# Turning q and k of seven head pairs on VectorE instead of TensorE, with a new order of short steps, in a block-sparse attention and Fourier-mixing kernel

## The chip, the cores and the metric

One Trainium2 chip, one NeuronCore. The time is the device time of one execution in microseconds (us). Most executions of one kernel lie within half a per cent of each other here: 42 of 44 runs of the kernel before in the four later jobs took 1108.34 to 1114.02 us at a granted TensorE clock of 0.991 to 0.995 of full speed; the two others took 1117.04 and 1117.07 us at 0.986. The kernel before had medians from 1109.45 to 1111.34 us on the chips of different jobs. So the clock differs a little from run to run, and kernels are compared by ratio: the mean time of one kernel's fast runs over that of the other's of the same rounds, which is not quite the ratio of the medians quoted beside it. A trace is of one execution, not always a typical one.

## The reference, cut to what matters

Four batches, eight heads, 768 positions, 64 features a head. Attention with a block mask (blocks of 32), then over the joined heads a two-dimensional Fourier transform of which the real part is added, a normalisation, and two dense layers with a relu.

```python
scores = scale * np.matmul(q, k.transpose(0, 1, 3, 2))   # q, k: (4, 8, 768, 64)
scores = np.where(mask, scores, -1e9)
attn = softmax(scores)                                   # rows; cut
x = np.matmul(attn, v)                                   # heads joined: (4, 768, 512)
u = x + np.real(np.fft.fft(np.fft.fft(x, axis=1), axis=2))
un = (u - mu) / np.sqrt(var + 1e-06)
out = u + np.maximum(un @ w_ch1, 0.0) @ w_ch2
```

## The kernel before: the parts that matter here

Two heads make a pair; there are 16 pairs, four a batch. A pair takes six steps (slots) of two score tiles each. While pair n is weighed, q and k of pair n + 1 are turned so that the features lie on partitions: twelve TensorE transposes into one shared PSUM bank ("t"), then copies. From the second batch on, the dense layers of the batch before fill the gaps of TensorE.

```python
def turn(n, a, half):                    # a: 0 for q, 1 for k
    ...
    for c, part in enumerate(parts):
        nc.tensor.transpose(tp[:, c * P:(c + 1) * P], part, ident)
    done = busy("PE", 0.15 * len(parts)) + HOP
    if a == 1:
        nc.scalar.copy(out=dst[:, half * HS:(half + 1) * HS], in_=tp[:, 0:HS])
        ...
    else:                                # q is put in the order even/odd, forward/backward
        for i, (to, to_jump, frm, jump, cnt, step) in enumerate(_TURNED[half]):
            on, copy = (("DVE", nc.vector.tensor_copy) if n == 0 and (half == 1 or i % 2 == 0)
                        else ("ACT", nc.scalar.copy))
            copy(out=_grid(dst, to, 2, to_jump, cnt, 1), in_=_grid(tp, frm, 2, jump, cnt, step))
```

The program is written out in advance against a small model of each engine's time (`when`, `free`, `busy`). Short steps (turns, copies of results, sums) wait in a list. `gap` takes those which the model holds ready; what is left is forced at the end of a slot.

```python
def slot(sl):
    ...                                  # scores, exponentials, values, products with gap()
    while short and (s in (2, 5) or len(short) > 1 or phase == 0 or sl == B * SB):
        short.popleft()[2]()             # first come, first served, ready or not
    ...                                  # loads of q and k
    w_steps(sl)                          # weight rounds of ACT and VectorE
```

## Time and profile before

| | value |
|---|---|
| time | 1109.45 us (1108.4 to 1109.46, 3 runs) |
| TensorE busy | 96% of the span; 99% from 300 to 1100 us |
| VectorE, ScalarE, GpSimd busy | 60%, 36%, 25% |
| TensorE at half clock in the trace | 16.2 us in four stretches, the last at the end |

A group's line gives source line, engine, operation, output and input with their shapes, count, then busy us and mean ns of one. PE is TensorE, PEld its weight loads, DVE is VectorE, ACT ScalarE, POOL GpSimd. In a timeline a line gives start, length, engine and group, and in brackets how long the engine stood idle before it and what ended that.

This is how the second half of pair 0's q (18.09) and of pair 1's q (22.90) is turned in the kernel before.

```profile
18.09 0.44 PE L447 MATMUL tp<-ident,qr 128*128 128x128 f32 x2 [1.12 <-ACT qT L456]
...
18.56 0.56 DVE L456 COPY qT<-tp 128x128 f32<-128x128 f32 x3 [7.51 <-PE tp L447]
...
20.63 0.43 DVE L414 TENSOR_SCALAR wraw<-wraw 128x512 uint32<-128x512 uint32 x1 [1.51 <-ACT wraw L413]
...
22.90 0.44 PE L447 MATMUL tp<-ident,qk 128*128 128x128 f32 x2
...
23.27 0.92 PE L478 MATMUL s<-qT,kT 64*128 64x384 f32 x4
```

VectorE copies q out of the bank at once (18.56) and starts on the weight round only after that (20.63); when TensorE comes to its next transposes the bank has long been free, and the line at 22.90 has no idle time before it.

### The profile page before, as it was taken

Reading aid. Unit: us, or ns where it says so; the run is one execution under the profiler, and the core shown is the slowest. Engines: PE = TensorE matmul, PEld = TensorE weight load, DVE = VectorE, ACT = ScalarE, POOL = GpSimd, SP = SyncE. Lnnn points to the kernel's source line nnn. Section 1 sums busy time; section 2 is a strip of 40 time slices with the busy share of each in tenths; the row PEclk is TensorE's granted clock in tenths of the full one; section 3 lists DMA queues with packets and bytes.
Section 4 is the critical chain, followed back from the end, with each engine's and each line's share of the span. In section 5 each row is a group of like instructions: output and inputs, shape, how many; then the busy total and the mean of one; then the engine's idle time right before and its main releaser. Section 6 shows DMA issues by size and latency. Waiting matters only on the chain.

```text
span 1109.3 us, 12468 instructions
## 1 busy us (share of the span) xinstructions
PE 1067.7 (96%) x4446; PEld 544.5 (49%) x4446; DVE 664.8 (60%) x1216; ACT 394.1 (36%) x818; POOL 274.2 (25%) x302
## 2 busy tenths in 40 slices
PE   8999988998899999999999999999999999999996
PEld 3333333544455545444444555454444555568675
DVE  5888878497754525653459355544356446575563
ACT  6788755555212102353443212244330202120210
POOL 1000088688100001245537000344540000000000
PEclk9999999999999999999999999999999999999999
DMA  7756311011000000211110000111000000100001
GB/s 219 208 176 215 93 51 43 15 45 42 1 1 1 0 1 19 66 33 27 43 29 15 1 0 1 51 50 29 1 1 0 1 1 19 39 1 1 1 16 45
DMA packets 65187, 44.30 MB, mean 40 GB/s; under 512 B 52814, under 2 KB 57948, under 8 KB 65116
## 3 DMA queue, kind: packets, MB, share of 16 engines
q1 hardware_dynamic: 63228, 42.62, 13.7%
q10 hardware_dynamic: 1856, 0.79, 0.3%
q8 instruction: 37, 0.61, 0.2%
q14 instruction: 34, 0.28, 0.1%
q0 software_dynamic: 32, 0.01, 0.0%
HBM read 37.11 MB, written 6.29 MB: 39 GB/s over the span
## 4 chain that ended last, share of the span: by engine, by line
PE 85%; DVE 9%; ACT 2%; issue 2%; DMA 0%; POOL 0%; SPq 0%; ACTq 0%; DVEq 0%; POOLq 0%
PE y L954 23%; PE z L898 15%; PE s L478 10%; PE o L522 9%; PE yp L898 7%; PE yy L1017 6%; PE xp L898 4%; DVE e L499 2%; PE tp L447 2%; PE zp L711 1%; PE sp L569 1%; PE zp L682 1%; PE xt L540 1%; PE s L483 1%; PE utp L823 1%
## 5 line engine op out<-in xcount | busy, mean ns | idle before, releaser
L509 POOL TENSOR_TENSOR acc<-acc,e 128x384 f32<-128x384 f32 x192 | 198.3, 1066 | 90.6 <-DVE e L499 90.1
L499 DVE TENSOR_TENSOR e<-s,mask 128x768 f32<-128x768 f32 x144 | 131.2, 951 | 78.4 <-ACT s L497 78.0
L478 PE MATMUL s<-qT,kT 64*128 64x384 f32 x768 | 161.7, 526 | 8.5 <-DVE e L499 7.4
L522 PE MATMUL o<-e,vr 128*64 128x384 f32 x768 | 145.1, 499 | 0.0
L497 ACT ACTIVATE s<-s 128x768 f32<-128x768 f32 x144 | 109.3, 795 | 65.5 <-PE s L478 64.9
L957 DVE TENSOR_TENSOR x<-y,x 128x512 f32<-128x512 f32 x72 | 49.8, 691 | 133.9 <-PE y L954 133.8
L954 PE MATMUL y<-w_sb,hB 128*128 128x512 f32 x288 | 128.4, 595 | 1.1 <-DVE x L957 1.0
L954 PE MATMUL y<-w_sb,hA 128*128 128x512 f32 x288 | 128.8, 594 | 0.6 <-ACT zs L713 0.6
L509 POOL TENSOR_TENSOR acc<-e 128x384 f32<-128x384 f32 x48 | 51.8, 1100 | 231.3 <-DVE e L499 173.2
L903 DVE TENSOR_TENSOR hA<-z,hA 128x384 f32<-128x384 f32 x64 | 35.7, 558 | 111.4 <-PE z L898 111.4
L478 PEld LDWEIGHTS s<-qT,kT 64*128 64x128 f32 x768 | 63.1, 187 | 68.1 <-DVE e L499 25.3
L898 PE MATMUL z<-unT,t 128*128 128x384 f32 x256 | 93.0, 486 | 0.0
L774 POOL TENSOR_SCALAR st<-st 128x1 f32<-128x1 f32 x24 | 6.6, 276 | 344.5 <-DVE st L773 344.1
L954 PEld LDWEIGHTS y<-w_sb,hB 128*128 128x128 f32 x288 | 53.3, 190 | 64.7 <-issue 62.1
L522 PEld LDWEIGHTS o<-e,vr 128*64 128x64 f32 x768 | 46.6, 136 | 73.9 <-issue 71.4
L954 PEld LDWEIGHTS y<-w_sb,hA 128*128 128x128 f32 x288 | 52.9, 190 | 59.6 <-issue 56.6
L907 ACT ACTIVATE hA<-hA 128x384 f32<-128x384 f32 x64 | 33.5, 524 | 123.6 <-DVE hA L903 123.1
L898 PEld LDWEIGHTS z<-unT,t 128*128 128x128 f32 x256 | 48.6, 190 | 33.9
L907 ACT ACTIVATE hB<-hB 128x384 f32<-128x384 f32 x64 | 33.6, 525 | 85.6 <-DVE hB L903 85.6
L898 PE MATMUL z<-t,w_sb 128*128 128x384 f32 x128 | 48.0, 499 | 3.1 <-DVE t L860 3.1
L898 PE MATMUL xp<-unT,w_sb 128*128 128x384 f32 x128 | 47.1, 491 | 1.5 <-ACT zs L713 1.1
L898 PE MATMUL yp<-unT,w_sb 128*128 128x384 f32 x128 | 46.7, 488 | 0.2 <-DVE un L747 0.2
(190 smaller groups left out, 1395.1 us busy)
## 6 DMA issues: line engine op xcount, KB each, us to landing
wraw<-in_moe_w_ch_dram SPq DMA_DIRECT2D x32, 512.0 KB
qr<-in_q_dram SPq DMA_DIRECT2D x90, 64.0 KB
vr<-in_v_dram SPq DMA_DIRECT2D x30, 192.0 KB
kr<-in_k_dram SPq DMA_DIRECT2D x28, 192.0 KB
out_dram<-x SPq DMA_DIRECT2D x16, 128.0 KB
out_dram<-x SPq DMA_DIRECT2D x8, 256.0 KB
out_dram<-x SPq DMA_DIRECT2D x8, 126.0 KB
out_dram<-x SPq DMA_DIRECT2D x4, 252.0 KB
```

The lines of the kernel that those rows point to most:

```text
L447: nc.tensor.transpose(tp[:, c * P:(c + 1) * P], part, ident)
L478: nc.tensor.matmul(s[:, i, 0:HS], kT[D * i:D * i + D, c * P:(c + 1) * P], qT[D * i:D * i + D, half * HS:(half + 1) * HS], start=True, stop ...
L497: nc.scalar.activation(out=s[:, :, 0:HS], in_=s[:, :, 0:HS], func=ACT.Exp, scale=scale)
L499: nc.vector.tensor_tensor(out=e, in0=s[:, :, 0:HS], in1=m.broadcast_to([P, 2, HS]), op=ALU.mult)
L509: nc.gpsimd.tensor_add(out=acc, in0=e_of[u - 1][:, i, :] if c == 1 else acc, in1=e[:, i, :])
L522: nc.tensor.matmul(o[D * i:D * i + D, :], vt[:, i, c, :], e[:, i, :], start=(c == 0), stop=(c == C - 1))
L898: nc.tensor.matmul(to, a[:, k, :], c[:, k, :], start=(k == 0), stop=(k == ND // 2 - 1))
L903: tt(out=to, in0=ps, in1=a, op=ALU.add)
L907: nc.scalar.activation(out=h, in_=h, func=ACT.Relu)
L954: nc.tensor.matmul(y, hs[0, half][:, l, m * P:(m + 1) * P], w2_sb[:, 4 * r + l, :], start=(l == 0), stop=(l == 3))
L957: nc.vector.tensor_tensor(out=x[:, m, :], in0=y, in1=x[:, m, :], op=ALU.add)
L1017: nc.tensor.matmul(ps, a[:, k, :], c[k // 2][:, k % 2, :] if isinstance(c, list) else c[:, k, :], start=(k == 0), stop=(k == 3))
```

## The change

Intent: take 84 transposes and their PSUM copies off TensorE and ScalarE. For pairs 9 to 15, q and k are loaded in blocks of 32 features by 32 positions (runs of 128 bytes), VectorE transposes the blocks in place, ScalarE puts q in order, and the scores read k with a stride of six columns. Beside that the first scores' copies all go to ScalarE, four warm-up matmuls are added, and short steps are taken in the order in which the model holds them ready. A limit with which the program compares the largest sum of squares also goes from 400 to 200. The core of the diff, with cuts marked:

```diff
+    BY_VECTOR = 2 * NP + 1
+    def load_blocks(n, a, tile):
+        ...
+            rows = (q, k)[a][b, 2 * j + i].rearrange("(t r) (g d) -> g r t d", r=BLK, d=BLK)
+            for g in range(D // BLK):
+                p0 = D * i + BLK * g
+                nc.sync.dma_start(
+                    out=tile[p0:p0 + BLK, :].rearrange("r (t d) -> r t d", d=BLK), in_=rows[g])
 ...
-                on, copy = (("DVE", nc.vector.tensor_copy) if n == 0 and (half == 1 or i % 2 == 0)
+                on, copy = (("DVE", nc.vector.tensor_copy) if n == 0 and half == 1
 ...
+    def flip_blocks(n, a):
+        t = loaded[n, a]
+        nc.vector.transpose(out=t, in_=t)
+    def in_order(n):
+        ...
+        for to, frm, *dims in _IN_ORDER:          # six copies
+            nc.scalar.copy(out=_at(qT, to, ...), in_=_at(t, frm, ...))
 ...
-            nc.tensor.matmul(s[:, i, 0:HS], kT[D * i:D * i + D, c * P:(c + 1) * P],
+            keys = kT[D * i:D * i + D, :]
+            nc.tensor.matmul(s[:, i, 0:HS],
+                             _run(keys, c, P, C) if n >= BY_VECTOR else keys[:, c * P:(c + 1) * P],
 ...
-        while short and (s in (2, 5) or len(short) > 1 or phase == 0 or sl == B * SB):
-            short.popleft()[2]()
+        while short and (s in (2, 5) or len(short) > 1 or phase == 0 or r == 0):
+            ready = [i for i in short if max(i[1], min(free[i[0]])) <= when["PE"] + 0.1]
+            if not ready and s not in (2, 5) and r > 0:
+                break
+            item = ready[0] if ready else short[0]
+            short.remove(item)
+            item[2]()
+        if BY_VECTOR <= n + 1 < len(pairs):
+            for at, fn, args in ((0, squares, (n + 1, 0)), (1, flip_blocks, (n + 1, 0)),
+                                 (2, in_order, (n + 1,)), (3, squares, (n + 1, 1)),
+                                 (4, flip_blocks, (n + 1, 1))):
 ...
-    warm(3)
+    warm(7)
```

## The prediction

> **What bounds the kernel now.** I read the page's table of engines first, then the chain that ended last, then busy time by stretches.
>
> ```profile
> span 1109.3 us, 12468 instructions
> PE 1067.7 (96%) x4446; PEld 544.5 (49%) x4446; DVE 664.8 (60%) x1216; ACT 394.1 (36%) x818; POOL 274.2 (25%) x302
> ...
> PE 85%; DVE 9%; ACT 2%; issue 2%; DMA 0%; POOL 0%; SPq 0%; ACTq 0%; DVEq 0%; POOLq 0%
> ```
>
> TensorE is busy for 96% of the span and holds 85% of the chain; no DMA is in it. An average can hide stages, so here are stretches (columns: busy us of PE, weight loads, DVE, ACT, POOL, each with its count; granted clock; DMA share; GB/s). The changed pairs, 9 to 15, are prepared from pair 8 on, that is between about 255 and 845 us.
>
> ```profile
> 100.00:255.00 155.00, 140.98 (x790) 59.26 (x786) 122.17 (x192) 92.79 (x195) 88.36 (x86) 0.98 0.24 66
> 255.00:300.00 45.00, 39.50 (x177) 20.53 (x176) 33.33 (x52) 17.87 (x37) 23.57 (x26) 0.96 0.07 18
> 300.00:430.00 130.00, 129.43 (x388) 68.53 (x388) 64.76 (x135) 20.74 (x46) 2.36 (x6) 1.00 0.00 1
> 430.00:620.00 190.00, 188.76 (x777) 87.46 (x777) 108.05 (x153) 73.10 (x152) 87.09 (x86) 1.00 0.13 34
> 700.00:845.00 145.00, 142.50 (x597) 65.92 (x596) 70.64 (x106) 54.61 (x107) 58.55 (x60) 1.00 0.08 22
> ```
>
> From 300 us on TensorE is over 98% busy while DVE is at 49 to 57%, ACT below 40%, DMA at 13% or less. There a TensorE instruction taken away shortens the span by what it occupied, and half a spare VectorE is there to take its work. From 100 to 300 us TensorE has about 20 us of holes and the clock is a little lower: that is where order can matter. One more view shows where VectorE itself is the limit, the chain of waits from 255 to 285 us (start, length, what):
>
> ```profile
> 272.76 0.80 ACT s L497
> ...
> 273.66 0.67 DVE e L499
> ...
> 274.53 0.95 DVE e L499
> 275.48 1.04 DVE un L786
> 276.52 1.42 DVE t L860
> ...
> 282.98 2.29 PE z L898 x3
> ```
>
> For 9 us, before the channel products of batch 1 start, TensorE waits for VectorE (with ACT and issue pieces between). This is the one place where more VectorE work costs time directly.
>
> [...] No VectorE transpose is in this trace. [...] loads of 64 columns take 136 ns and of 128 columns 187 to 190 ns, so 64 columns cost 51 to 54 ns[...]; there is a constant of some 80 ns beside it. [...] The new scores read keys every sixth float, 24 bytes apart[...]. No load in this trace is strided so; it cannot say.
>
> **The change part by part.**
>
> *Removed on TensorE.* Twelve 128 by 128 transposes per pair (six of q, six of k), 84 for seven pairs. They are these in the stretch 255 to 845 us (PE, weight loads, DVE, ACT):
>
> ```profile
> 255.00:845.00 590.00, 14.71 (x84) 9.47 (x84) 0.00 (x0) 17.16 (x77) 1.00 0.07 19
> ```
>
> 14.7 us overcounts, because matmul records overlap. I took each group in the raw trace from the start of its first transpose to the start of the next other matmul. Pure groups take 0.28 to 0.59 us (two transposes 0.28 to 0.37, three 0.33 to 0.51, four 0.44 to 0.53). Added per pair 9 to 15: 3.07 + 1.51 + 1.57 + 1.76 + 2.41 + 1.52 + 1.57 = 13.4 us. In this are two waits for the one PSUM bank that the transposes share: 1.4 us in pair 9 and 0.84 us in pair 13. The first is this one:
>
> ```profile
> 262.36 0.60 PE tp L447 x4
> ...
> 262.99 0.61 ACT qT L456 x3
> ...
> 263.62 0.40 ACT qT L456 x3
> ...
> 264.07 0.44 PE tp L447 x2
> ```
>
> Both go with their cause, so I take off the whole 13.4 us: **-13.4**.
>
> *ACT.* Removed per pair: nine copies of q, 3 x 0.270 + 3 x 0.275 + 3 x 0.174 = 2.16 us, and two of k, 2 x 0.478 = 0.96 us; 3.1 x 7 = 21.8 us. Added: six copies of q, two each of 256, 126 and 2 elements. From 128 elements (0.270) and 384 (0.478) a slope of 0.81 ns per element gives 0.37 for 256, so 2 x (0.37 + 0.27 + 0.17) = 1.6 us a pair, 11.5 us in all. The squares stay (0.85 us, same number). ACT falls by about 10 us and is not the bound: **0**.
>
> *VectorE.* Added: 14 transposes in place of 768 floats. One-source work of 512 elements takes 0.60 us here and two-source work of 768 takes 0.95; I take 0.9, so 12.6 us. In the stretches past 300 us it lies in idle time. Two of them (pair 9) fall in 255 to 283 us, where VectorE heads the chain shown above: **+1.8**.
>
> *TensorE, scores of the seven pairs.* 42 steps of two units; in the raw trace eight weight loads and eight matmuls of each step go in four waves, two row halves side by side. The first wave takes 0.43 us to the next, later ones 0.32. So 0.105 us of the first load is exposed, the rest hidden. If the stride halves the streaming part (107 ns becomes 214), the hidden loads still fit in 322 ns and only the first costs, 42 x 0.107 = 4.5 us. I give this about a half: **+2.2**.
>
> *DMA.* q and k of a changed pair now come in 128-byte runs in place of 256: 6144 packets in place of 3072. In the trace a 256-byte packet takes 18 ns of an engine and a 4-byte one 9, so I estimate 13 to 14 ns for 128 bytes: 6144 x 13.5 / 16 = 5 us per pair, over 16 engines, and a pair lasts 36 to 40 us where these loads are made. A k load of 1536 packets lands about 3 us after its first packet; 3072 would take 6. The first user of k comes one step earlier than before (ACT in step 3 in place of TensorE in step 4), of q in step 0 rather than 1; they still have about three steps of 3.4 us or more: **0**.
>
> *Order.* The very first scores: all six copies of q's first half on ACT (about 1.4 us after each other) where ACT and DVE shared them; in exchange VectorE no longer sits 7.5 us waiting for them before the mask rows. Four more warm-up matmuls fill a wait. Together within 0.5 us. Short steps are now taken in order of readiness, and an unready one is left where it was forced before. In pairs 4 to 8 TensorE waits for such steps (x copies 3.2 + 1.3, q 1.1, by the waits from 100 to 255 us), against 7.2 us in front of scores on VectorE, which order of short steps hardly touches. Draining all of them at each batch's first step may force a wait for POOL's sums. I take half of the 5.6 us less 1: **-2**. The new limit changes a comparison only.
>
> Sum: -13.4 + 1.8 + 2.2 - 2 = -11.4; 1109.45 - 11.4 = **1098 us**.
>
> **The rivals.** (a) *The strided weight load becomes a bound.* If it slowed fourfold, a load (over 0.43 us) would no longer fit in a wave of 0.32 and each of 42 x 4 waves would grow by 0.1 to 0.2 us: 17 to 34 us lost, and the result is 1115 to 1130. For it: [...] no strided load in the trace. Against it: two row halves load at once and three of four waves have over 0.1 us to spare. (b) *VectorE or ACT becomes late.* The flip stands in VectorE's queue in front of the mask product or a channel addition. 0.9 us late 14 times, all exposed, gives back 12.6 us: about 1109, no change. Against it: the products fill TensorE past 300 us, and waits of TensorE on VectorE between 255 and 845 us are some 6 us. (c) *Short runs land late.* Loads wait in one queue in order, behind stores that wait for VectorE. A late q or k would hold ACT, then scores: 2 to 5 us a pair, 14 to 35 us. Against it: DMA is 0% of the chain and 13% busy. (d) *Order gains more.* If most of the 11 us of TensorE holes between 100 and 255 us closed and the clock there rose, the time would be 1086 to 1090.
>
> **Range and chances.** (a) to (c) at moderate strength push to 1106; (d) with a free stride to 1088. So 1098, 8 in 10 from 1088 to 1106. Faster by over 2% means below 1087.7, which needs (d) in full with no cost of stride: 0.09. Slower by over 2% needs (a) or (c) at full strength: 0.03. Within 2%: 0.88.
>
> **What would show it.** Right: transposes on L447's counterpart fall from 192 to 108; TensorE's instructions to about 4366; 14 VectorE transposes of about 0.9 us; ACT near 384 us, DVE near 677; TensorE still over 98% busy from 300 us; weight loads of scores in the seven pairs at 186 to 300 ns; DMA still 0% of the chain. Wrong: such loads over 0.4 us with waves apart by more than 0.33 us (a); new waits of scores or values on the VectorE transpose (b); ACT's squares waiting for a DMA (c); far fewer TensorE waits before 255 us (d).

## The result, and the profile after

The changed kernel took 1116.96 us (1112.58 to 1118.05, 4 runs), ratio to before 1.0063 (95% interval 1.0034 to 1.0091). In another job it took 1115.91 us, ratio 1.0036 (1.0019 to 1.0053). It is slower by about half a per cent; the prediction of 1098 us, with a range of 1088 to 1106, was wrong.

The page after: the table of engines, and the chain that ended last.

```profile
span 1116.1 us, 12285 instructions
PE 1072.0 (96%) x4370; PEld 557.2 (50%) x4370; DVE 669.3 (60%) x1227; ACT 389.5 (35%) x786; POOL 271.2 (24%) x302
...
PE 86%; DVE 8%; issue 2%; ACT 2%; POOL 1%; ACTq 0%; DVEq 0%; POOLq 0%
```

TensorE has 76 instructions fewer (84 transposes off, 8 records of warm-ups on) and still 4.3 us more busy time. So part of what is left takes longer. The stretches (same columns as in the prediction):

```profile
255.00:300.00 45.00, 37.35 (x168) 17.96 (x169) 34.90 (x54) 20.18 (x39) 28.00 (x32) 0.92 0.11 23
...
430.00:620.00 190.00, 187.79 (x738) 94.10 (x737) 108.99 (x153) 71.78 (x135) 85.20 (x86) 1.00 0.16 34
...
700.00:845.00 145.00, 140.95 (x572) 71.10 (x571) 73.74 (x117) 52.67 (x96) 60.81 (x66) 1.00 0.11 25
```

From 430 us on TensorE is nearly as full as before (98.8% against 99.3% of the first of these two stretches, 97.2% against 98.3% of the second), VectorE has room, DMA is at 16% or less, and weight loads have grown from 87.5 to 94.1 us in the first of the two though there are 40 fewer.

The most useful comparison was the start of each pair's first score matmul in the raw traces, as the difference to the kernel before:

```
                 pair 0   pair 1   pair 4   pair 5   pair 8   pair 9   pair 13  last result copy
after            -0.74    +6.20    +2.93    +6.64    +7.23    +6.82    +5.21    +6.77 us
```

It splits the question in two. Some 7 us are lost before pair 8, most of it before pair 1 starts, where no turn has changed yet. And from pair 9 on, where the prediction saw about 10 us of gain for TensorE, nothing is gained in the end. The first loss is in this timeline, which answers to the one of before:

```profile
18.38 0.44 PE L483 MATMUL tp<-ident,qr 128*128 128x128 f32 x2
18.42 0.43 DVE L450 TENSOR_SCALAR wraw<-wraw 128x512 uint32<-128x512 uint32 x1 [8.70 <-ACT wraw L449]
...
23.78 0.69 DVE L458 TENSOR_TENSOR w_sb<-w_sb,wraw 128x512 f32<-128x512 f32 x1
24.39 0.55 DVE L492 COPY qT<-tp 128x128 f32<-128x128 f32 x3
25.04 0.66 PE L483 MATMUL tp<-ident,qk 128*128 128x128 f32 x2 [3.99 <-issue]
25.63 1.65 PE L538 MATMUL s<-qT,kT 64*128 64x384 f32 x4
```

Pair 0's q is turned at 18.38 as before, but its copies stand in VectorE's queue behind two weight rounds and run at 24.39; TensorE's next transposes, which need the same bank, start after 3.99 us of idle time ("issue" means that the view names no releaser). The four score matmuls after it take 1.65 us where they took 0.92 before: TensorE is at half clock. The trace's clock records hold 10.24 us at 0.5 from 23.8 us on; in all 36.4 us at half clock against 16.2 before.

### The profile page after: what moved, and what is told of

The parts are those of the page before. It is cut to its first block, busy times and chain, and to the rows that moved or that the text cites.

```text
span 1116.1 us, 12285 instructions
## 1 busy us (share of the span) xinstructions
PE 1072.0 (96%) x4370; PEld 557.2 (50%) x4370; DVE 669.3 (60%) x1227; ACT 389.5 (35%) x786; POOL 271.2 (24%) x302
## 4 chain that ended last, share of the span: by engine, by line
PE 86%; DVE 8%; issue 2%; ACT 2%; POOL 1%; ACTq 0%; DVEq 0%; POOLq 0%
PE y L1015 23%; PE z L959 15%; PE s L538 11%; PE o L583 9%; PE yp L959 7%; PE yy L1078 6%; PE xp L959 4%; DVE e L560 3%; PE zp L772 1%; PE sp L630 1%; POOL acc L570 1%; PE tp L483 1%; PE zp L743 1%; PE xt L601 1%; PE s L544 1%
## 5 line engine op out<-in xcount | busy, mean ns | idle before, releaser
L538 PE MATMUL s<-qT,kT 64*128 64x384 f32 x768 | 170.3, 549 | 11.8 <-DVE e L560 11.6
L583 PE MATMUL o<-e,vr 128*64 128x384 f32 x768 | 148.1, 508 | 0.0
L538 PEld LDWEIGHTS s<-qT,kT 64*128 64x128 f32 x768 | 82.0, 240 | 71.9 <-DVE e L560 33.8
L979 ACT COPY hA<-xp 128x384 f32<-128x384 f32 x32 | 15.3, 479 | 98.3 <-PE xp L959 98.3
```

Of the source, the lines that this page charges most:

```text
L538: nc.tensor.matmul(s[:, i, 0:HS], _run(keys, c, P, C) if n >= BY_VECTOR else keys[:, c * P:(c + 1) * P], qT[D * i:D * i + D, half * HS:(ha ...
L583: nc.tensor.matmul(o[D * i:D * i + D, :], vt[:, i, c, :], e[:, i, :], start=(c == 0), stop=(c == C - 1))
L979: nc.scalar.copy(out=h11, in_=x)
```

## The experiments

Theory A: the loss is made of the new order (that wait and the clock behind it) and of the strided weight load; the turn on VectorE by itself gains. Rival B: the turn on VectorE costs its own gain, by late VectorE or ScalarE work. Ratios are to the kernel before in the same rounds.

### The VectorE turn alone

The changed kernel with the old first scores and short steps first come, first served. The old condition could not be kept to the letter, so the list is drained at each batch's first step (up to pair 8 its pairs start within 0.13 us of the kernel before's).

```diff
-            ready = [...]; if not ready and s not in (2, 5) and r > 0: break; ...
+            short.popleft()[2]()          # condition: ... or phase == 0 or r == 0
-                on, copy = (("DVE", ...) if n == 0 and half == 1
+                on, copy = (("DVE", ...) if n == 0 and (half == 1 or i % 2 == 0)
-    warm(7)
+    warm(3)
```

> The kernel before with the VectorE turn of pairs 9 to 15 alone (short steps first come first served as before, only drained at each batch's first step, without which the check finds a conflict; first scores as before). Theory A: the loss lies in the new order (a 4 us wait of TensorE at 21 us and 10 us of halved clock behind it), and the turn by itself gains 13.4 us of transposes less 4.6 us of strided weight loads less some 3 us of waits on ACT's reordering and VectorE: 1102 to 1106 us. Rival B: the turn itself eats its whole gain or more: 1109 us or above.

Measured: 1110.67 us (1107.42 to 1114.86), ratio 1.0000 (0.998 to 1.002); in the trace the last result copy comes 1.9 us earlier than before. A miss for A's number and nearer to B's: the turn by itself is worth nothing that the runs can tell. What it is made of the further runs show.

### The short-step rule alone, and the first scores alone

The rule alone: the kernel before with the new `while` loop. The first scores alone: the kernel before with the copies of q's first half on ScalarE and `warm(7)`.

> The kernel before with the new rule for short steps alone. Theory A: the second half of q of pair 0 is again put off, its copies stand in VectorE's queue behind two weight rounds, TensorE waits some 4 us near 21 us and gets half the clock for up to 10 us after: 1112 to 1118 us, clock below before's. Rival B: 1107 to 1110 us, no wait over 2 us before 100 us.

> The kernel before with the change at the first scores alone (all copies of q's first half on ACT, seven warm-up matmuls), short steps and turns as before. Theory: it moves the first scores by 0.7 us and nothing else: within 1.5 us of before. Rival: it is part of the loss: 3 us or more above before.

Measured: the rule 1117.58 us, ratio 1.0069 (1.0045 to 1.0093), last result copy 7.8 us later, and 10.24 us of half clock from 24.2 us on; the first scores 1111.41 us, ratio 1.0002 (0.9986 to 1.0017). So the rule carries the whole loss of the changed kernel, and the first scores carry none.

### The three copies moved from VectorE to ScalarE

In the changed kernel, only the copies of the second half of pair 0's q change engine. TensorE's instructions are the same, in the same order.

```diff
-                on, copy = (("DVE", nc.vector.tensor_copy) if n == 0 and half == 1
+                on, copy = (("ACT", nc.scalar.copy) if n == 0 and half == 1
```

> The changed kernel with only the three copies of the second half of pair 0's q moved from VectorE to ACT; TensorE's order is the same, instruction by instruction. Theory A: the 4 us wait at 21 us goes (below 1 us) and with it the halved clock at 24 to 34 us: 5 to 7 us off the changed kernel, 1110 to 1112 us. Rival B (the wait is bound to something else, ACT's queue or the weights' loads): 1115 us or above, wait still there.

Measured: 1107.74 us (1107.49 to 1109.41), ratio 0.9973 (0.9961 to 0.9986): 7 to 10 us off the changed kernel (by its two ratios), more than the 5 to 7 expected, through three copies of half a microsecond in all. The wait of 3.99 us is down to 0.34 (bracket of the second line of this timeline of the experiment):

```profile
20.65 0.51 ACT L492 COPY qT<-tp 128x128 f32<-128x128 f32 x3
...
21.21 0.44 PE L483 MATMUL tp<-ident,qk 128*128 128x128 f32 x2 [0.34 <-ACT qT L492]
```

The half clock at 24 us is gone, pair 1 starts 1.7 us earlier than before where it was 6.2 later, and at pair 8 this kernel is 3.3 us ahead of before. Of these 3.3 us 0.9 are there at pair 0's first scores already; that start differs by -0.9 to +1.8 us between traces of kernels that are alike up to it, so it is no gain of the rule. The other 2.4 us are what the new rule gains in the first 250 us, once it does not cause this wait (the moved copies under the old rule were not run).

### The wait filled with idle matmuls

To part the wait from the clock: the copies stay on VectorE, and 16 matmuls of the identity into a spare score tile stand in front of the delayed transposes.

```diff
     def turn(n, a, half):
+        if (n, a, half) == (1, 0, 1): 16 x nc.tensor.matmul(fill[:, 0, 0:P], ident, ident, ...)
```

> The changed kernel with 16 idle matmuls put where TensorE stands for 4 us at 21 us; the copies stay on VectorE, so the next transposes still start at about 25 us, but TensorE is not idle before. It parts the wait from the clock. Theory: some 4 us of the 10 that the copies on ACT won are the wait, the rest the halved clock[...]: the 10.24 us at half clock at 24 us are gone from the records, and the time is 4 to 7 us under the changed kernel, 1109 to 1112 us. Rival (the clock falls for another reason, or costs nothing): within 2 us of the changed kernel.

Measured: 1110.28 us (1107.79 to 1112.05), ratio 0.9983 (0.996 to 1.0005). The windows of 15 to 45 us of before, after, the copies on ScalarE and the filled wait show it (the number after POOL's count is the granted clock):

```profile
15.00:45.00 30.00, 28.88 (x182) 10.03 (x178) 21.72 (x41) 23.93 (x52) 0.00 (x0) 1.00 0.78 235
```
```profile
15.00:45.00 30.00, 26.01 (x141) 8.78 (x135) 18.33 (x34) 17.91 (x39) 0.00 (x0) 0.83 0.63 192
```
```profile
15.00:45.00 30.00, 29.66 (x188) 10.45 (x180) 22.86 (x41) 25.78 (x56) 0.00 (x0) 1.00 0.80 245
```
```profile
15.00:45.00 30.00, 29.78 (x195) 13.04 (x195) 18.15 (x34) 20.91 (x46) 0.00 (x0) 1.00 0.67 208
```

After, only 141 matmuls start in these 30 us, at a mean clock of 0.83; with the wait filled the clock stays at 1.00. From pair 0's to pair 1's first scores it takes 36.4 us in the changed kernel, 32.5 with the wait filled, 28.6 with the copies moved. So by pair 1's start about 3.9 us are the wait and 3.8 us the clock it brings down. This rests on one trace of each; the times of the whole kernels with the wait filled and with the copies moved (ratios 0.9983 and 0.9973) can't be told apart.

Most half-clock records of these traces are 3.41 us long, and those of one trace start whole multiples of 3.41 us apart. TensorE was not idle all through the stretches before them: the record of 10.24 us starts at 23.79, 2.7 us into the wait of 3.99, after 3.41 us in which TensorE was 20% busy, and in the kernel before the records at 190.59 and 248.62 us each follow 3.41 us in which it was 43% busy. In the 14 traces, before each kernel's end, every fall to half clock follows 3.41 us with TensorE at most 56% busy; some windows of this raster with 48 to 56% were followed by none.

What the clock costs can be estimated from the traces as half of TensorE's busy time inside half-clock records. From pair 0's to pair 8's first scores (us):

| kernel | all | TensorE idle | lost to the clock |
|---|---|---|---|
| before | 239.7 | 15.7 | 1.7 |
| after | 247.7 | 16.5 | 9.6 |
| copies on ScalarE | 237.3 | 13.2 | 1.7 |

So in the trace nearly all of the changed kernel's loss up to pair 8 is the clock; the idle time of the one wait is nearly balanced by waits that the new rule takes away elsewhere.

### Keys loaded so that the scores read them contiguously

In the changed kernel the rows of k are loaded, by the same 128-byte runs, in the order of the scores' key blocks. All instruction orders stay.

```diff
-  k[...].rearrange("(t r) (g d) -> g r t d", r=BLK, d=BLK)
+  k[...].rearrange("(u r t) (g d) -> g r t u d", r=BLK, t=C, d=BLK)   # into "r (t u d)", u=4
-  _run(keys, c, P, C) if n >= BY_VECTOR else keys[:, c * P:(c + 1) * P]
+  keys[:, c * P:(c + 1) * P]
```

> The changed kernel with the rows of k of pairs 9 to 15 brought in the order of the scores' key blocks by the same 128-byte runs, so that the weight loads of the scores read contiguous columns; all instruction orders are the same. Theory A: the loads fall from 294 to 186 ns, the first wave of each of 42 steps from 0.537 to 0.427 us, 4.6 us off the changed kernel: about 1112 us. Rival: the longer load is hidden elsewhere (the next group starts later anyway), under 2 us off.

Measured: 1112.28 us (1111.7 to 1113.9), ratio 1.0011 (0.9998 to 1.0025). The weight loads of the scores from 450 to 845 us, of before, after and this run:

```profile
L478 PEld LDWEIGHTS s<-qT,kT 64*128 64x128 f32 x328 | 27.4, 185 | 31.4 <-issue 13.3 <-DVE e L499 6.3 <-DVE hB L903 2.5
```
```profile
L538 PEld LDWEIGHTS s<-qT,kT 64*128 64x128 f32 x336 | 46.4, 300 | 28.5 <-issue 13.3 <-DVE e L560 11.0 <-DVE hA L964 1.6
```
```profile
L538 PEld LDWEIGHTS s<-qT,kT 64*128 64x128 f32 x336 | 27.8, 185 | 38.4 <-issue 14.4 <-DVE e L560 12.2 <-DVE hB L964 2.5
```

185, 300, 185 ns. In the raw trace the first of the four waves of each of the 42 steps grew from 0.427 to 0.537 us and was at 0.427 again in this run, the later ones stayed at 0.32: 42 x 0.110 = 4.6 us. The trace of this run ends 4.0 us before the changed kernel's. Theory A holds here.

### Both corrections together, and with the VectorE transposes left out

The copies on ScalarE and the contiguous keys in one kernel; and the same without `nc.vector.transpose` (a wrong result).

> The changed kernel with both corrections: the three copies on ACT and the keys contiguous. If the two effects add (each measured alone: about 10 and 6 us off the changed kernel): 1100 to 1104 us, ratio to before 0.991 to 0.995. If they share a cause: 1105 to 1108 us.

> As b1, without the 14 VectorE transposes (wrong result on purpose; all other instructions in the same order). Theory: VectorE's 13 us are hidden but for the place near 280 us: 0 to 2.5 us off b1. Rival: VectorE's later mask products cost each time: 4 us or more off b1.

Measured: both together 1104.52 us (1101.36 to 1107.11), ratio 0.9943 (0.9915 to 0.9971), correct, faster than both kernels; without the VectorE transposes 1103.99 us, ratio 0.9939. The two corrections add up, and the VectorE work is hidden. The two times alone would not show that (each interval is some 3 us wide to either side, and 1.8 us were predicted), but the traces do: from pair 9's to pair 15's first scores TensorE is idle for 5.2 us with the VectorE transposes and for 5.2 us without. From pair 8's to pair 9's it is idle for 6.1 us without them, and for 6.1 us with them in the trace with the filled wait, whose half-clock records fall at the same places (7.5 us in the trace of both corrections, where they fall elsewhere). So 14 instructions like these (count, then shortest, median and longest in ns, of k's tile in the changed kernel) cost nothing that shows.

```profile
L511 DVE STREAM_TRANSPOSE kT<-kT x7: 962/967/969, 279.9 to 792.2; 128x768 f32<-128x768 f32 x7
```

### The transposes and copies left out, with nothing in their place

To measure the largest term of the prediction: the kernel before, where pairs 9 to 15 use pair 8's turned q and k (a wrong result).

```diff
-            nc.tensor.transpose(tp[:, c * P:(c + 1) * P], part, ident)
+            n > 8 or nc.tensor.transpose(tp[:, c * P:(c + 1) * P], part, ident)   # copies likewise
```

> The kernel before with the transposes and copies of pairs 9 to 15 left out and nothing in their place (these pairs take pair 8's turned q and k; wrong result on purpose). It measures the term that the prediction took as 13.4 us. Theory: 12 to 14 us off before, about 1097 us. Rival: a group's worth is less than from its start to the next start, because the next group then pays its own first weight load or a wait: 7 to 10 us off, 1100 to 1103 us.

Measured: 1104.82 us (1102.44 to 1110.06), ratio 0.9948 (0.9917 to 0.9979), the trace 7.1 us shorter than before's. This is the rival's side, and by the ratio even a little less than its 7 to 10 us: all of TensorE's and ScalarE's turning of seven pairs is worth 6 to 7 us, not 13.4. By the starts of the pairs, pair 9's removal (3.07 us in the prediction) gained nothing, pairs 10, 11, 12 and 13 gained 1.6, 1.2, 1.2 and 2.2 us, pair 14 (1.52) nothing, pair 15 1.2. For pair 9 the chain of waits tells why (start, length, what):

```profile
275.51 1.04 DVE un L788
276.55 1.41 DVE t L862
...
282.53 0.44 DVE t L862
...
283.01 1.01 PE z L900
```

It is the VectorE chain that the prediction shows, at the very same times: its product starts at 283.01 here and at 282.98 in the kernel before. TensorE came earlier, and lost what it had won in front of that chain: it waited 2.10 us for scores, which it did not in the kernel before, and had half the clock from 272.76 to 276.17 us (timeline of TensorE):

```profile
271.55 2.22 PE L480 MATMUL s<-qT,kT 64*128 64x384 f32 x8 [2.10 <-DVE e L501]
```

In pair 13, where pair 14 is prepared, 0.93 us of waiting for scores appeared in place of the transposes; the rest of its loss I did not trace.

### ScalarE's reordering of q in two halves

In the trace after, ScalarE's six copies take 1.86 us in a run (predicted 1.6) and stand in front of the next exponentials. In pair 13 TensorE then waits 1.61 us for scores. The chain there:

```profile
740.66 0.32 ACT qT L521
...
742.23 0.20 ACT qT L521
742.42 0.71 ACT s L558
...
743.22 0.97 DVE e L560
...
744.24 1.88 PE s L538 x7
```

Two splits were tried on the kernel with both corrections. One later: three copies in step 2, three in step 3, squares and flip of k each a step later. One earlier: flip of q in step 0, copies in steps 1 and 2, k untouched.

```diff
-  (0, squares q), (1, flip q), (2, in_order), (3, squares k), (4, flip k)
+  (0, squares q), (1, flip q), (2, in_order 0), (3, in_order 1), (4, squares k), (5, flip k)   # later
+  (0, squares q), (0, flip q), (1, in_order 0), (2, in_order 1), (3, squares k), (4, flip k)   # earlier
```

> As b1, with ACT's reordering of q cut in two (three copies in step 2, three in step 3; squares and flip of k one step later). Theory: the 1.86 us run of copies ahead of the exponential is what made TensorE wait 0.7 and 1.6 us for scores in pairs 10 and 13, so these waits fall below 0.5 us: 1 to 2.5 us off b1. Rival: new waits take their place, within 1 us of b1.

> As b1, with ACT's reordering of q cut in two and moved forward (flip of q at the end of step 0, three copies in step 1, three in step 2), so that no load and no deadline of k moves. Theory: TensorE's wait of 1.6 us for scores in pair 13 falls below 0.7 us, the 0.7 us one in pair 11 (behind ACT's squares of k) stays; 1 to 2 us off b1 in the same rounds, and none of the long waits of the split into later steps. Rival: the split is again slower than b1 by 5 us or more, because the copies' place and not their length matters.

Measured: later 1140.53 us, ratio 1.0254 (1.0225 to 1.0283); earlier 1103.57 us (1100.24 to 1105.28), ratio 0.9931 (0.9916 to 0.9946). The later split is a clear miss. Who waited for whom in it (total us, times, longest):

```profile
PE s L537 <- DVE e L559: 21.2, 14, 8.8
PE s L537 <- issue: 10.7, 3, 6.4
PE s L537 <- DVE kT L511: 8.7, 4, 3.0
```

The flip of k in the last step is too late for the next pair's scores (third line). The wait of 8.8 us lies behind a ScalarE copy into x that stood until a store of the old x had landed, with q's second copies and the exponentials queued behind it. The edit moved the reordering, the flip and the loads that depend on them at once, so how the 36 us divide, and why that store was late, is not settled. The earlier split halved the wait in pair 13 (1.72 to 0.84 us in the two traces) and made one of 0.96 us in pair 9; it can't be told from the kernel with both corrections. Either of the two is the best version here.

### The changed kernel once more

> The changed kernel again, in the rounds of the others: 1112 to 1118 us, ratio to before 1.004 to 1.009.

Measured: 1115.91 us, ratio 1.0036, as told above; its trace has the same pattern (+6.5 us at pair 1, +7.0 at the end, 10.24 us of half clock at 24.1 us).

## Why the prediction was wrong

By its own terms, with what the runs showed:

| term | predicted | measured |
|---|---|---|
| transposes and copies off | -13.4 | -7.1 in the trace, ratio 0.9948 |
| VectorE transposes on | +1.8 | 0 (idle time of TensorE the same; 0.9943 with, 0.9939 without) |
| strided weight loads | +2.2 | +4.6 by the waves, 4.0 by the traces' ends |
| ScalarE, DMA | 0 | +0.6 as the rest of the turn alone (-1.9 + 7.1 - 4.6) |
| order | -2 | +7.8 for the rule, 0 for the first scores |
| sum | -11.4 | +5.9 from these; +6.8 in the trace |

The fourth row is a rest, and it hides a cost. From pair 9's to pair 15's first scores TensorE is idle for 2.5 us in the kernel before and for 4.9 with the turn alone; nearly all of these 2.4 us are two waits for scores, the one of 1.6 us in pair 13 behind ScalarE's copies and one of 0.7 us in pair 11. The prediction had 0 for it.

**The step that failed first is the order.** The prediction wrote: "an unready one is left where it was forced before", and counted only TensorE waits that could go: "I take half of the 5.6 us less 1: -2". It did not ask what a step that is left ends up behind. Left one slot, the second half of pair 0's q came after that slot's weight rounds; its copies, on VectorE, stood behind 6 us of other work, and the bank they free is the one that the next transposes need. The prediction had named a forced wait at the batches' first steps as the risk, which is another place. The halved clock was in none of its terms. The half of the idea that was right: without this wait the kernel gains 2.4 us from pair 0's to pair 8's first scores, about the 2 us predicted. Later, too, waits count twice: from pair 4 to 5 the changed kernel loses 3.7 us with two half-clock records (143 and 153 us), the one with the copies moved 1.1 us with none.

**The second is the size of the largest term.** "Both go with their cause, so I take off the whole 13.4 us". The prediction itself showed that from 275 to 283 us VectorE holds the chain, and charged VectorE's added work there, but did not strike out pair 9's 3.07 us, which lie in front of that same chain; the run without the turn shows none of it gained. It also read that chain as "For 9 us, ... TensorE waits for VectorE": in these 9.3 us TensorE stands for 4.4 us (1.28 and 3.10) and works for the rest. For the other pairs it counted from a group's start to the next start, on the ground that "a TensorE instruction taken away shortens the span by what it occupied"; removed alone, pairs 11, 12, 13 and 15 gave 0.2 to 0.6 us less than counted, and pair 14 nothing. (Two small slips that change nothing: seven times its 1.62 us of ScalarE copies are 11.3 us, not 11.5, and the holes of 100 to 255 us in rival (d) are 14.0 us by its own stretches, not 11.)

**Strided weight loads**: the size was right. With the streaming part of a load doubled ("107 ns becomes 214") the estimate was 293 ns for a load; measured 300, against 185 contiguous, with only the first wave exposed (0.537 against 0.427 us). The 107 ns agree with the trace before, where 64 columns more cost 51 to 54 ns (136 and 187 to 190 ns), so 128 columns 102 to 108; the doubling was the estimate, and no run shows what slows the load. Only the weight of a half was wrong: the whole 4.5 us came, give or take 0.5. Rival (a), a fourfold load, did not.

**VectorE and DMA**: a transpose takes 0.967 us (0.9 predicted) and is hidden; rival (b) falls by the run without the flips. In the changed kernel's list of waits no ScalarE square waits for a load, and a 128-byte packet takes 13 ns in the raw trace (median of 43,008), as estimated; rival (c) falls. (d) falls too.

What is not settled: about 1 us between the sum of the terms and the trace. Part of it lies in where the half-clock records fall. Against the kernel before, pair 9's start gains 0.4 us on pair 8's in the changed kernel, 2.0 with the turn alone, and 3.4 with the wait filled and without the flips, both of which have the new rule. By the estimate above TensorE's idle time and the clock take 7.5 and 3.3, 6.0 and 3.3, and 6.1 and 1.4 us there, and the rest is the same to 0.3 us. So a gain of 2 to 3 us in one trace can be the place of these records; no run moved them on purpose.

## What to carry to other kernels

Before counting a removed instruction as time won, look for the next place where its engine waits for another: what is removed ahead of that wait moves into it. When an order rule lets a step slip, list the queue that its last instruction will then stand in, and who needs what it frees. Look at TensorE's idle time per window of 3.4 us and not only at its longest wait, and fill it with idle matmuls if need be: here every fall to half clock followed a window in which TensorE was 56% busy or less, one wait of 4 us cost nearly 8 by the next pair's start, and with 16 idle matmuls in it the granted clock of 15 to 45 us was 1.00 and not 0.83.

## What was measured of the hardware

- TensorE's weight load for the scores, 64 rows by 128 fp32 columns, took 185 ns contiguous (before, and the run with the keys contiguous) and 300 ns with columns 24 bytes apart (after), means from 450 to 845 us. Of four waves of loads only the first showed it (0.537 against 0.427 us).
- A VectorE transpose in place of 128 partitions by 768 fp32 took 967 ns (962 to 969, seven of k, after).
- Records of half clock followed windows of 3.41 us in which TensorE was 43% (before, the record at 190.59 us) and even 56% busy (after, at 143.25 us). And one wait of 3.99 us brought 10.24 us of half clock, of which 9.0 us fell on matmuls that were dense again, about as dear as the wait itself (3.8 and 3.9 us).
- A DMA packet took 13 ns for 128 bytes (median of 43,008, after) and 18 ns for 256 (median of 49,152, before) in the raw trace.
